# Dividing the last octet's head outputs instead of its softmax weights, with a new order of work

## The chip, the cores and the metric

The kernel runs on one core of one Trainium2 chip. The metric is the device time of one execution in microseconds (us), the median of several runs. Engines are named as the profile names them: PE (TensorE, matrix products; PEld is its weight load), DVE (VectorE), ACT (ScalarE), POOL (GpSimd) and SP (SyncE, which here issues nearly all DMAs). PSUM is the memory into which PE accumulates, in 8 banks; SBUF holds everything else.

## The reference, cut to what matters

A recurrent attention layer with 8 memory rows runs over 2048 tokens in 64 segments of 32, one after the other: each segment needs the memory that the one before it made. Beside it stands a gated feed-forward layer on the same tokens, and a gate mixes the two.

```python
for s in range(n_seg):                       # 64 segments, in order
    h = concatenate([mem, x[:, 32*s:32*s+32]])      # 8 + 32 = 40 rows, 640 wide
    q, k, v = h @ Wq, h @ Wk, h @ Wv         # 32 heads of 192
    scores = where(mask, q @ k.T * scale, -1e9)
    p = softmax(scores)                      # over 40 keys
    o = (p @ v) @ Wo                         # sum over the heads
    mem = o[:, :8]                           # the next segment's memory
    outs.append(o[:, 8:])
g = sigmoid((x * gate_w).sum(-1))
return g * concatenate(outs) + (1 - g) * (gelu(x @ w_gate) * (x @ w_up)) @ w_down
```

## The kernel before, in words

The feed-forward layer is done first, in about the first tenth of the time. The 64 segments follow, and this is what the change touches.

**Heads and octets.** The 32 heads are taken eight at a time: four *octets* per segment, numbered 0 to 3 in the order of work (even segments take the heads upwards, odd ones downwards). Weights do not all fit into SBUF. Of the pieces of the first and last octet, 13 of W_q, W_k and W_v (384 KB each) and 3 of W_o (480 KB each) share their places: when a piece has been used, SP loads its partner into the same place (`swap_loads`), for use later in the same segment. SP issues these DMAs in order, among its other loads and stores.

**Left rows.** The last 8 tokens of each segment do not depend on the memory. Their Q and K are computed for four segments and one octet at once (a *left group*: `left_mm`, LQ and LK), evicted by ACT (`left_rows`, L889), transposed by DVE (L891) and stored to DRAM; their V (`vl_mm`, Vl) and output product (`wo_left`, Wol) are likewise made for four segments at once. Which left group falls to a segment depends on its number modulo 4; segments with remainder 3 have none, but carry the Wol products, those with remainder 0 carry most of Vl.

**One octet's steps.** The projections (`proj`) are PE matmuls in groups of four that run side by side in 32-column tiles, k = 0 to 4 along the 640; ACT evicts rows and V, DVE transposes the rows of Q and K into place (`row_transp`, L1080), POOL adds the left rows (`left_fill`, L941 and L943). `scores` writes the mask and the products to a PSUM bank; DVE takes the maximum and subtracts it. `softmax`: ACT's exp (L1124), then on DVE the sum (L1126), its reciprocal (L1128), and two products that write p in two parts, 32 main keys (L1130) and 8 left keys (L1131). `p_transp` transposes p on PE (L1144, L1149); for the last octet ACT evicts the main part and DVE the other (L1158). `pv_oct` multiplies by V (L1177, L1179); ACT evicts the head outputs u (L1188), for the last octet DVE does a third of it (L1193); POOL copies the left rows of u aside (L1196). `wo_part` multiplies by W_o: octets 0 to 2 add up in one PSUM bank (L1206), whose two halves `half_sums` adds on ACT and DVE (L1212, L1215); the last octet has a bank of its own (L1229, twelve groups of four matmuls).

**End of a segment.** DVE adds the two (L1371), transposes the new memory into the next segment's input (L1375), in two parts each, and then mixes in the gate and the feed-forward part (L975). The next segment's first projection needs that transposition.

**Order.** Each engine executes its own instructions in the order in which the program adds them, and waits on semaphores that follow from the regions each step reads and writes (`_Sched`). The order is the list `PROG`, written out as a literal list, the same for all segments: ("g", n, k) a projection group of `GROUPS[n]`, ("tq" | "tk", o) the row transpositions, ("sc", o) scores, ("ex", o) softmax, ("pt", o) transposition of p, ("pv", o) the product with V, ("wo", o, half) the output product, ("lf" / "le", remainder, unit, k or m) a left group's matmuls and evictions in segments with that remainder, ("vb", k) the left V of the next segment. Left evictions that stand behind the last ("wo", 3, 1) are added after the end of the segment.

Of the kernel before, what the change touches and what calls it, by code (L numbers as in the profile page):

```python
# [3 lines left out]
ACTF = mybir.ActivationFunctionType  # L4
ALU = mybir.AluOpType
# [226 lines left out]
def _build(nc, A_x, A_mem0, A_Wq, A_Wk, A_Wv, A_Wo, seg_len, w_gate, w_up, w_down,  # L232
# [140 lines left out]
    r_ident = sreg(wsA_off["ident"], 256)  # L373
    maskm = bview(wsA_off["maskm"], R * 2)
# [125 lines left out]
    def piece_view(key, o):  # L500
        if key[0] == 3:
# [4 lines left out]
    PROG = [("g", 0, 0), ("g", 0, 1), ("g", 0, 2), ("g", 0, 3), ("g", 0, 4), ("tq", 0), ("g", 1, 0), ("tk", 0),  # L506
# [610 lines left out]
    def softmax(s, o):  # L1117
# [14 lines left out]
        if o == NOCT - 1:  # L1132
            for fn, rp in zip(fns, r_pp):
                S_.add("dve", fn, reads=[rb, rst], writes=[rp], name="smax p")
# [336 lines left out]
```

## Time and profile before

| | |
|---|---|
| median of 3 runs | 1765.9 us (1765.88 to 1769.65) |
| the profiled execution | 1766.88 us, span 1765.1 us |
| PE busy | 1623.9 us (92%) |
| DVE, ACT, POOL busy | 960.0, 802.8, 320.0 us (54%, 45%, 18%) |
| DMA | 499.57 MB, mean 283 GB/s |
| granted PE clock | 0.994 of full speed |

The span runs from the first to the last instruction of the profiled execution; the execution's own time is 1.8 us longer. Busy time is the union of an engine's instructions. "Idle before" is the time that an engine stood still just before an instruction, with what ended it.

### The profile page before, as it was taken

The page shows a single profiled execution, that of the slowest core. Times are in us where ns is not written, and L with a number is a line of the kernel's source. Part 1 is how long each engine was busy: PE and PEld are TensorE (multiplying, and loading weights), DVE is VectorE, ACT ScalarE, POOL GpSimd, SP SyncE. Part 2 cuts the span into 40 slices and gives each one's busy share as a digit, 9 for nine tenths or more (in the row PEclk, how much of TensorE's full clock was granted, in tenths as well). Part 3 has the DMA queues.
Part 4 walks back from the last instruction along what each step waited for, and adds up shares of the span by engine and source line. Part 5 has one row for each costly group of instructions (what it writes and reads, how often), then busy time and mean ns, then how long its engine had stood idle before and what let it go on. Part 6 is the DMA issues. An engine that isn't in the chain of part 4 may idle for free.

```text
span 1765.1 us, 80301 instructions
## 1 busy us (share of the span) xinstructions
PE 1623.9 (92%) x39162; PEld 809.5 (46%) x31501; DVE 960.0 (54%) x2932; ACT 802.8 (45%) x1835; POOL 320.0 (18%) x1099
## 2 busy tenths in 40 slices
PE   9999999999999999999999989999999998999887
PEld 4554444444444444454444444454444444454444
DVE  2222655556555655555555655555555655655554
ACT  3222544545444544444444544444444544445443
POOL 1100111111112112111212111111211121121211
PEclk9999999999999999999999999999999999999999
DMA  9814987888778887888788887879787886879776
GB/s 335 295 48 157 329 313 250 320 313 288 280 269 311 299 308 253 315 290 319 281 280 293 296 293 250 314 285 323 279 280 275 311 310 241 312 282 327 283 275 238
DMA packets 271311, 499.57 MB, mean 283 GB/s; under 512 B 105304, under 2 KB 132208, under 8 KB 270960
## 3 DMA queue, kind: packets, MB, share of 16 engines
q1 hardware_dynamic: 267832, 491.34, 78.3%
q8 instruction: 276, 4.52, 1.0%
q10 hardware_dynamic: 3128, 3.09, 0.6%
q14 instruction: 75, 0.61, 0.1%
HBM read 473.22 MB, written 21.11 MB: 280 GB/s over the span
## 4 chain that ended last, share of the span: by engine, by line
PE 71%; DVE 15%; DMA 6%; issue 4%; ACT 4%; DVEq 0%; SPq 0%; ACTq 0%
PE ps L1046 20%; PE ps L226 15%; PE ps L1206 8%; DMA arena<-in_A_Wo_dram 5%; PE ps L1177 3%; PE ps L804 3%; PE ps L801 3%; PE ps L884 3%; PE ps L1100 3%; PE ps L819 2%; PE ps L1087 2%; DVE ps L1114 2%; DVE arena L1112 2%; PE ps L1095 2%; PE ps L1229 2%
## 5 line engine op out<-in xcount | busy, mean ns | idle before, releaser
L1046 PE MATMUL ps<-arena 128*32 128x384 bf16 x9940 | 723.0, 329 | 42.4 <-DVE arena L1375 34.4
L226 PE MATMUL ps<-arena 128*32 128x384 bf16 x7680 | 595.4, 328 | 7.9 <-DVE arena L1215 3.5
L1046 PEld LDWEIGHTS ps<-arena 128*32 128x32 bf16 x9940 | 257.5, 97 | 365.3 <-issue 226.0
L1080 DVE STREAM_TRANSPOSE arena<-arena 128x384 bf16<-128x384 bf16 x512 | 270.8, 557 | 150.8 <-ACT arena L1066 149.2
L1066 ACT ACTIVATE arena<-ps 128x384 bf16<-128x384 f32 x512 | 236.2, 489 | 211.6 <-PE ps L1046 196.3
L1206 PE MATMUL ps<-arena 128*32 128x320 bf16 x6144 | 293.6, 301 | 13.9 <-issue 13.4
L1124 ACT ACTIVATE ps<-ps 104x160 f32<-104x160 f32 x256 | 71.9, 281 | 293.4 <-DVE ps L1114 293.4
L1206 PEld LDWEIGHTS ps<-arena 128*32 128x32 bf16 x6144 | 163.5, 97 | 74.0 <-issue 19.4
L1112 DVE TENSOR_REDUCE arena<-ps 104x4 f32<-104x160 f32 x256 | 83.0, 324 | 165.8 <-PE ps L1100 164.6
L941 POOL COPY arena<-arena 128x96 bf16<-128x96 bf16 x256 | 70.3, 275 | 513.4 <-PE ps L1100 444.2
L1188 ACT ACTIVATE arena<-ps 128x480 bf16<-128x480 f32 (+1 forms) x256 | 137.0, 535 | 43.8 <-PE ps L1179 39.6
L1196 POOL COPY arena<-arena 128x96 bf16<-128x96 bf16 x256 | 68.3, 267 | 441.1 <-ACT arena L1188 357.3
L1162 ACT ACTIVATE arena<-ps 128x448 bf16<-128x448 f32 x192 | 104.2, 543 | 96.7 <-PE ps L1149 96.4
L1069 ACT ACTIVATE arena<-ps 128x384 bf16<-128x384 f32 x256 | 125.1, 489 | 20.9 <-PE ps L1046 16.3
L1177 PE MATMUL ps<-arena 128*64 128x160 bf16 x1536 | 123.1, 243 | 12.5 <-ACT arena L1162 6.9
L1126 DVE TENSOR_REDUCE arena<-ps 104x4 f32<-104x160 f32 x256 | 83.0, 324 | 92.5 <-ACT ps L1124 92.5
L1177 PEld LDWEIGHTS ps<-arena 128*64 128x64 bf16 x1536 | 80.8, 109 | 91.6 <-issue 31.7
L884 PE MATMUL ps<-arena 128*32 128x384 bf16 x1280 | 111.4, 330 | 2.2 <-issue 2.0
L1179 PE MATMUL ps<-arena 128*64 128x64 bf16 x1536 | 104.8, 193 | 4.1 <-issue 4.1
L891 DVE STREAM_TRANSPOSE arena<-arena 128x384 bf16<-128x384 bf16 x128 | 73.7, 576 | 31.6 <-ACT arena L889 27.8
L1215 DVE TENSOR_TENSOR arena<-ps,arena 64x160 f32<-64x160 f32 x160 | 50.8, 317 | 72.3 <-ACT arena L1212 61.6
L1114 DVE TENSOR_TENSOR ps<-ps,arena 104x160 f32<-104x160 f32 x256 | 85.0, 332 | 8.8
(84 smaller groups left out, 1819.2 us busy)
## 6 DMA issues: line engine op xcount, KB each, us to landing
arena<-in_A_Wk_dram SPq DMA_DIRECT2D x335, 384.0 KB, 7.1
arena<-in_A_Wv_dram SPq DMA_DIRECT2D x335, 384.0 KB, 9.1
arena<-in_A_Wo_dram SPq DMA_DIRECT2D x205, 480.0 KB, 6.4
arena<-in_A_Wq_dram SPq DMA_DIRECT2D x209, 384.0 KB, 5.4
arena<-left_qk_scratch SPq DMA_DIRECT2D x126, 96.0 KB, 2.8
left_qk_scratch<-arena SPq DMA_DIRECT2D x49, 192.0 KB, 2.3
left_qk_scratch<-arena SPq DMA_DIRECT2D x30, 96.0 KB, 5.7
ffn_b_scratch<-arena ACTq DMA_DIRECT2D x16, 160.0 KB, 4.4
```

The source lines that it names most:

```text
L226: return e.add_instruction(mybir.InstMatmult(name=nm, start_tensor_calc=like["start"], stop_tensor_calc=stop, tile_size=(128, 32), tile_po ...
L884: fns.append(lambda e, outp=outp, rhs=rhs, j=j: e.matmul(outp, lhs, rhs, start=(k == 0), stop=(k == KT - 1), tile_position=(0, 32 * j)))
L1046: fns.append(lambda e, outp=outp, rhs=rhs, j=j: e.matmul(outp, lhs, rhs, start=(k == 0), stop=(k == KT - 1), tile_position=(0, 32 * j)))
L1066: S_.add("act", lambda e, m=m, bk=bk: e.activation(out=rows_sb[m], in_=ps[:, bk, 0:384], func=ACTF.Copy), reads=[r_ps[bk]], writes=[r_rows ...
L1069: S_.add("act", lambda e, i=i, bk=bk: e.activation(out=v_sb[i % NVB].rearrange("p (c n) -> p c n", c=3), in_=ps[:, bk, 0:384].rearrange("p ...
L1080: S_.add("dve", lambda e: e.transpose(out=dst[:, :, 0:L], in_=rows_sb[m].rearrange("p (c r) -> p c r", r=L)), reads=[r_rows[m]], writes=[r ...
L1112: S_.add("dve", lambda e: e.tensor_reduce(out=mxs, in_=S3, axis=AX.X, op=ALU.max), reads=[rb], writes=[rst], name="smax max")
L1114: S_.add("dve", lambda e: e.tensor_tensor(out=S3, in0=S3, in1=mxb, op=ALU.subtract), reads=[rb, rst], writes=[rb], name="smax sub")
L1177: return [lambda e: e.matmul(full, v[:, e0:e0 + 64], PTm[:, i], start=True, stop=False, tile_position=(0, 64 * i), skip_group_check=True), ...
L1179: lambda e: e.matmul(part, vl[:, e0:e0 + 64], PTl[:, i], start=False, stop=True, tile_position=(0, 64 * i), skip_group_check=True)]
L1188: S_.add("act", lambda e: e.activation(out=apx(u[:, 0, 0, :], [[R, na], [3 * R, 4], [1, R]]), in_=ps[:, A, 0:na * W].rearrange("p (c t r) ...
L1206: fns.append(lambda e, i=i, t=t, j=j, gv=gv: e.matmul(ps[32 * j:32 * j + 32, bank, 0:2 * DJ].rearrange("p (h n) -> p h n", h=2), lhs2[i], ...
```

## The change

For the last octet alone, exp now writes p itself, unnormalised, in its two parts (two ACT instructions); the DVE sum, reciprocal and products of that octet are gone. A column of ones (beside the mask in SBUF) times the transposed p gives each row's sum on PE, in every one of the 64 rows that the head outputs of that tile take ("PVn"). DVE takes the reciprocal of these sums, 128x160, from PSUM into the place of K's rows. The product with V is split into two PE steps (PVa, PVb), and DVE evicts both with a multiplication by the reciprocals ("uT norm", 128x320; "uT norm2", 128x160), where ACT and DVE each copied one before. POOL's copy of the left rows follows both. The last octet's W_o matmuls are ordered by the thirds c of a head pair: c = 0 and 1 of a half's pairs first, and c = 2 of all four pairs at the very end. The half sums of octets 0 to 2 become an item of the order, ("hs", 0), which stands behind ("pv", 3). `PROG` is new throughout.

```diff
--- before.py
+++ after.py
@@ -371,6 +371,10 @@
     r_gallL = sreg(wsA_off["gallL"], 128)
     ident = bview(wsA_off["ident"], 256)
     r_ident = sreg(wsA_off["ident"], 256)
+    assert R * 2 + 2 <= wsA["maskm"]
+    ones = bview(wsA_off["maskm"] + R * 2, 2).broadcast_to([128, 64])
+    r_ones = sreg(wsA_off["maskm"] + R * 2, 2)
+    rcp, r_rcp = fview(wsB_off["K"], 16 * R), sreg(wsB_off["K"], 16 * R)
     maskm = bview(wsA_off["maskm"], R * 2)
     r_maskm = sreg(wsA_off["maskm"], R * 2)
 
@@ -503,20 +507,20 @@
         return bview(o, GQ)
 
     GROUPS = [[(0, 0), (1, 0)], [(2, 0), (0, 1), (1, 1)], [(2, 1), (0, 2)], [(1, 2)], [(2, 2), (0, 3)], [(1, 3)], [(2, 3)]]
-    PROG = [("g", 0, 0), ("g", 0, 1), ("g", 0, 2), ("g", 0, 3), ("g", 0, 4), ("tq", 0), ("g", 1, 0), ("tk", 0),
-            ("g", 1, 1), ("g", 1, 2), ("sc", 0), ("g", 1, 3), ("ex", 0), ("g", 1, 4), ("tq", 1), ("g", 2, 0),
-            ("g", 2, 1), ("g", 2, 2), ("lf", 1, 0, 0), ("pt", 0), ("g", 2, 3), ("tk", 1), ("g", 2, 4), ("g", 3, 0),
-            ("sc", 1), ("g", 3, 1), ("lf", 1, 0, 1), ("g", 3, 2), ("ex", 1), ("g", 3, 3), ("g", 3, 4), ("g", 4, 0),
-            ("lf", 1, 0, 2), ("pv", 0), ("lf", 1, 0, 3), ("g", 4, 1), ("tk", 2), ("g", 4, 2), ("pt", 1), ("g", 4, 3),
-            ("tq", 2), ("g", 4, 4), ("sc", 2), ("ex", 2), ("lf", 1, 0, 4), ("pv", 1), ("g", 5, 0), ("le", 1, 0, 0),
-            ("g", 5, 1), ("lf", 0, 1, 0), ("g", 5, 2), ("wo", 0, 0), ("le", 1, 0, 1), ("tq", 3), ("pt", 2), ("g", 5, 3),
-            ("wo", 0, 1), ("g", 5, 4), ("pv", 2), ("tk", 3), ("lf", 0, 1, 1), ("lf", 1, 1, 0), ("wo", 1, 0), ("sc", 3),
-            ("lf", 2, 1, 0), ("wo", 1, 1), ("g", 6, 0), ("lf", 2, 1, 1), ("lf", 1, 1, 1), ("g", 6, 1), ("ex", 3),
-            ("g", 6, 2), ("wo", 2, 0), ("lf", 1, 1, 2), ("pt", 3), ("g", 6, 3), ("lf", 2, 1, 2), ("g", 6, 4),
-            ("wo", 2, 1), ("lf", 2, 1, 3), ("lf", 1, 1, 3), ("pv", 3), ("lf", 0, 1, 2), ("lf", 2, 1, 4), ("lf", 1, 1, 4),
-            ("vb", 0), ("le", 1, 1, 0), ("vb", 1), ("vb", 2), ("vb", 3), ("le", 1, 1, 1), ("le", 2, 1, 0),
-            ("lf", 0, 1, 3), ("lf", 0, 1, 4), ("wo", 3, 0), ("le", 2, 1, 1), ("le", 0, 1, 0), ("wo", 3, 1), ("le", 0, 1, 1),
-            ("vb", 4)]
+    PROG = [("g", 0, 0), ("g", 0, 1), ("g", 0, 2), ("g", 0, 3), ("g", 0, 4), ("tq", 0), ("g", 1, 0), ("g", 1, 1),
+            ("tk", 0), ("g", 1, 2), ("sc", 0), ("g", 1, 3), ("ex", 0), ("g", 1, 4), ("g", 2, 0), ("g", 2, 1),
+            ("tq", 1), ("g", 2, 2), ("g", 2, 3), ("tk", 1), ("pt", 0), ("g", 2, 4), ("sc", 1), ("ex", 1),
+            ("pv", 0), ("lf", 1, 0, 0), ("g", 3, 0), ("g", 3, 1), ("lf", 1, 0, 1), ("g", 3, 2), ("lf", 1, 0, 2),
+            ("g", 3, 3), ("g", 3, 4), ("tq", 2), ("tk", 2), ("g", 4, 0), ("g", 4, 1), ("g", 4, 2), ("pt", 1),
+            ("g", 4, 3), ("g", 4, 4), ("g", 5, 0), ("g", 5, 1), ("sc", 2), ("lf", 1, 0, 3), ("lf", 1, 0, 4),
+            ("lf", 0, 1, 0), ("ex", 2), ("pv", 1), ("lf", 0, 1, 1), ("le", 1, 0, 0), ("le", 1, 0, 1), ("tq", 3),
+            ("wo", 0, 0), ("pt", 2), ("g", 5, 2), ("g", 5, 3), ("g", 5, 4), ("wo", 0, 1), ("wo", 1, 0), ("pv", 2),
+            ("tk", 3), ("sc", 3), ("wo", 1, 1), ("lf", 1, 1, 0), ("g", 6, 0), ("wo", 2, 0), ("lf", 2, 1, 0),
+            ("g", 6, 1), ("ex", 3), ("lf", 1, 1, 1), ("pt", 3), ("lf", 2, 1, 1), ("lf", 2, 1, 2), ("g", 6, 2),
+            ("lf", 1, 1, 2), ("g", 6, 3), ("lf", 0, 1, 2), ("g", 6, 4), ("wo", 2, 1), ("pv", 3), ("lf", 1, 1, 3),
+            ("vb", 0), ("lf", 1, 1, 4), ("vb", 1), ("lf", 0, 1, 3), ("hs", 0), ("lf", 2, 1, 3), ("lf", 2, 1, 4),
+            ("le", 1, 1, 0), ("le", 1, 1, 1), ("lf", 0, 1, 4), ("le", 0, 1, 0), ("vb", 2), ("vb", 3), ("wo", 3, 0),
+            ("le", 2, 1, 0), ("wo", 3, 1), ("vb", 4), ("le", 0, 1, 1), ("le", 2, 1, 1)]
     assert NOCT == 4
     WOP = 4
     NWP = NT
@@ -648,6 +652,7 @@
                                                  base=base, channel_multiplier=cm), reads=[reg], writes=[reg])
 
     S_.add("pool", lambda e: e.memset(maskm, 0.0), writes=[r_maskm])
+    S_.add("pool", lambda e: e.memset(bview(wsA_off["maskm"] + R * 2, 2), 1.0), writes=[r_ones])
     asel(maskm[:, 0:XA], r_maskm, [[-1, XA]], 0, 1, NEG)
     asel(maskm[:, L:R], r_maskm, [[-1, M]], -L, 1, NEG)
     asel(maskm[:, L:R], r_maskm, [[0, M]], -L, 1, 0.0)
@@ -1121,6 +1126,13 @@
         rst = r_st[o % 2]
         rcb = rcs.rearrange("p (t o) -> p t o", o=1).broadcast_to([104, 4, R])
         rb = r_ps[bank]
+        if o == NOCT - 1:
+            q = s % 4
+            for dst, src, rp in ((pm_sb[0:104], S3[:, :, 0:L], r_pp[0]),
+                                 (pl_sb[0:104, :, M * q:M * q + M], S3[:, :, L:R], r_pp[1])):
+                S_.add("act", lambda e, dst=dst, src=src: e.activation(out=dst, in_=src, func=ACTF.Exp, bias=0.0, scale=scale),
+                       reads=[rb], writes=[rp], name="smax exp")
+            return
         S_.add("act", lambda e: e.activation(out=S3, in_=S3, func=ACTF.Exp, bias=0.0, scale=scale),
                reads=[rb], writes=[rb], name="smax exp")
         S_.add("dve", lambda e: e.tensor_reduce(out=sms, in_=S3, axis=AX.X, op=ALU.add),
@@ -1129,11 +1141,7 @@
         q = s % 4
         fns = [lambda e: e.tensor_tensor(out=pm_sb[0:104], in0=S3[:, :, 0:L], in1=rcb[:, :, 0:L], op=ALU.mult),
                lambda e: e.tensor_tensor(out=pl_sb[0:104, :, M * q:M * q + M], in0=S3[:, :, L:R], in1=rcb[:, :, L:R], op=ALU.mult)]
-        if o == NOCT - 1:
-            for fn, rp in zip(fns, r_pp):
-                S_.add("dve", fn, reads=[rb, rst], writes=[rp], name="smax p")
-        else:
-            S_.add("dve", fns, reads=[rb, rst], writes=[r_p], name="smax p")
+        S_.add("dve", fns, reads=[rb, rst], writes=[r_p], name="smax p")
 
     def p_transp(s, o):
         bank = 5 + o % 2
@@ -1179,6 +1187,34 @@
                     lambda e: e.matmul(part, vl[:, e0:e0 + 64], PTl[:, i], start=False, stop=True,
                                        tile_position=(0, 64 * i), skip_group_check=True)]
 
+        if o in USPLIT:
+            def sums(i):
+                return [lambda e: e.matmul(ps[64 * i:64 * i + 64, B, 0:W], ones, PTm[:, i], start=True, stop=False,
+                                           tile_position=(0, 64 * i), skip_group_check=True),
+                        lambda e: e.matmul(ps[64 * i:64 * i + 64, B, 0:W].rearrange("p (t r) -> p t r", r=R)[:, :, XA:R], ones,
+                                           PTl[:, i], start=False, stop=True, tile_position=(0, 64 * i), skip_group_check=True)]
+
+            def both(x, y):
+                return [z for xy in zip(x, y) for z in xy]
+
+            vr = [r_v[o % NVB], r_vl[oc], r_PT]
+            S_.add("pe", both(sums(0), sums(1)), reads=[r_PT, r_ones], writes=[r_ps[B]], name="PVn s%d o%d" % (s, o))
+            S_.add("dve", lambda e: e.reciprocal(out=rcp, in_=ps[:, B, 0:W]), reads=[r_ps[B]], writes=[r_rcp], name="PV rcp s%d" % s)
+            S_.add("pe", both(half(0, 0), half(0, 1)) + both(half(1, 0), half(1, 1)), reads=vr, writes=[r_ps[A]], name="PVa s%d o%d" % (s, o))
+            S_.add("pe", both(half(2, 0), half(2, 1)), reads=vr, writes=[r_ps[B]], name="PVb s%d o%d" % (s, o))
+            S_.add("dve", lambda e: e.tensor_tensor(
+                out=apx(u[:, 0, 0, :], [[R, 2], [3 * R, 4], [1, R]]),
+                in0=ps[:, A, 0:2 * W].rearrange("p (c t r) -> p c t r", t=4, r=R), in1=apx(rcp, [[0, 2], [R, 4], [1, R]]),
+                op=ALU.mult), reads=[r_ps[A], r_rcp], writes=[ru[0]], name="uT norm s%d o%d" % (s, o))
+            S_.add("dve", lambda e: e.tensor_tensor(
+                out=u[:, :, 2, :], in0=ps[:, B, 2 * W:3 * W].rearrange("p (t r) -> p t r", r=R),
+                in1=rcp.rearrange("p (t r) -> p t r", r=R), op=ALU.mult),
+                reads=[r_ps[B], r_rcp], writes=[ru[1]], name="uT norm2 s%d o%d" % (s, o))
+            q = s % 4
+            S_.add("pool", lambda e: e.tensor_copy(
+                out=uTl[:, 12 * oc:12 * oc + 12, M * q:M * q + M].rearrange("p (t c) i -> p t c i", c=3), in_=u[:, :, :, L:R]),
+                reads=[r_uT[o % NUB]], writes=[r_uTl[oc]], name="uTl s%d o%d" % (s, o))
+            return
         fns = [x for c in range(3) for y in zip(half(c, 0), half(c, 1)) for x in y]
         if s % 4 == 0:
             S_.add("pe", fns[:2], reads=[r_v[o % NVB], r_PT], writes=[r_ps[A]], name="PV s%d o%d" % (s, o))
@@ -1216,6 +1252,8 @@
                 out=zsum[64 * h:64 * h + 64], in0=ps[0:64, bank, DJ * h:DJ * (h + 1)], in1=zpart[0:64, DJ * h:DJ * (h + 1)],
                 op=ALU.add), reads=[r_ps[bank], r_zp], writes=[r_zp], name="Zs " + tag)
 
+    late_wo = []
+
     def wo_part(s, item):
         ub = item[1] % NUB
         u = uT[ub]
@@ -1224,21 +1262,22 @@
         allp = wo_pairs(s, ("wo", NOCT - 1)) if lasto else [p for i in range(NOCT - 1) for p in wo_pairs(s, ("wo", i))]
         held = [(p,) + piece(s, (3, p)) for p in pairs]
         if lasto:
-            for p, g_, rg_ in held:
-                for c in range(3):
-                    S_.add("pe", [lambda e, j=j, c=c, g_=g_, p=p: e.matmul(
-                        ps[32 * j:32 * j + 32, OB2, SC:512], u[:, p % 4, c, 0:L], g_[:, c, DJ * j:DJ * (j + 1)],
-                        start=(p == allp[0] and c == 0), stop=(p == allp[-1] and c == 2),
-                        tile_position=(0, 32 * j)) for j in range(4)],
-                        reads=[rg_, r_uT[ub]], writes=[r_ps[OB2]], name="Wo s%d p%d" % (s, p))
+            late_wo.extend(held)
+            end = pairs[-1] == allp[-1]
+            for c, (p, g_, rg_) in [(c, x) for c in range(2) for x in held] + [(2, x) for x in late_wo if end]:
+                S_.add("pe", [lambda e, j=j, c=c, g_=g_, p=p: e.matmul(
+                    ps[32 * j:32 * j + 32, OB2, SC:512], u[:, p % 4, c, 0:L], g_[:, c, DJ * j:DJ * (j + 1)],
+                    start=(p == allp[0] and c == 0), stop=(p == allp[-1] and c == 2),
+                    tile_position=(0, 32 * j)) for j in range(4)],
+                    reads=[rg_, r_uTp[ub][c // 2]], writes=[r_ps[OB2]], name="Wo s%d p%d" % (s, p))
+            if end:
+                late_wo.clear()
             return held
         for (pa, ga, ra), (pb, gb, rb) in zip(held[::2], held[1::2]):
             for c in range(3):
                 S_.add("pe", wo_split(OB, [u[:, pa % 4, c, 0:L], u[:, pb % 4, c, 0:L]], [ga[:, c, :], gb[:, c, :]],
                                       pa == allp[0] and c == 0, pb == allp[-1] and c == 2),
                        reads=[ra, rb, r_uT[ub]], writes=[r_ps[OB]], name="Wo s%d p%d" % (s, pa))
-        if pairs[-1] == allp[-1]:
-            half_sums(OB, "s%d" % s)
         return held
 
     def wo_left(s, held):
@@ -1251,7 +1290,7 @@
 
     assert PROG.index(("g", [n for n, ms in enumerate(GROUPS) if (2, 1) in ms][0], KT - 1)) < PROG.index(("wo", 0, 0))
     late_at = ("g", 1, KT - 1)
-    items = [item for item in PROG if item[0] not in ("lf", "le", "vb")]
+    items = [item for item in PROG if item[0] not in ("lf", "le", "vb", "hs")]
     n_wo = PROG.index(items[-1])
     assert PROG.index(("sc", 2)) < PROG.index(("pv", 1))
     assert wsB["K"] >= 768
@@ -1331,6 +1370,8 @@
                     for m in range(2):
                         LBK[m] = lb[item[2], m]
                     left_mm(*unit(s, item[2]), item[3], unit_piece)
+            elif kind == "hs":
+                half_sums(OB, "s%d" % s)
             elif kind == "vb":
                 if q == 3 and g + 1 < NG:
                     if i == 0:
```

## The prediction, made before the result was known

> **What bounds the kernel now.** I read the page first, then the groups of instructions with shapes kept apart, the list of waits, and the chain of waits across the end of one segment. The page:
>
> ```profile
> PE 1623.9 (92%) x39162; PEld 809.5 (46%) x31501; DVE 960.0 (54%) x2932; ACT 802.8 (45%) x1835; POOL 320.0 (18%) x1099
> ```
>
> TensorE is busy 92% of the span, so a shorter VectorE chain pays only where TensorE waits for it. The waits (engine and line, what it waited for, us in total, times, longest):
>
> ```profile
> PEld ps L1144 <- DVE arena L1131: 84.6, 155, 1.0
> ...
> PE ps L1046 <- DVE arena L1375: 34.4, 48, 1.2
> PE ps L1144 <- DVE arena L1131: 25.0, 65, 0.7
> ...
> PE ps L1229 <- DMA arena<-in_A_Wo_dram: 6.1, 10, 2.3
> ```
>
> L1144 is the transposition of p, L1375 the new memory's transposition that lets the next segment begin. In the trace the 64 segments start (first Q matmul, L1046) on average 24.70 us apart: by number mod 4, called the kind from here, 25.16, 25.07, 23.42 and 25.21 for kinds 0 to 3. Now the chain of waits across the end of a kind 2 segment (start, us, what):
>
> ```profile
> 939.32 0.59 DVE arena L891
> ...
> 940.01 0.58 DVE arena L891
> 940.59 0.16 DVE arena L1371
> ...
> 940.77 0.26 DVE arena L1375
> ...
> 941.07 0.35 PE ps L1046 x4
> ```
>
> and two lines of the timeline of the same stretch:
>
> ```profile
> 938.95 0.31 DVE L1193 CAST arena<-ps 128x160 bf16<-128x160 f32 x1
> 939.32 1.13 PE L1229 MATMUL ps<-arena 128*32 128x160 bf16 x48
> ```
>
> The last 48 output matmuls end at 940.45, yet L1371, which adds them up, starts at 940.51: VectorE's two left transposes (L891) ran until 940.58. VectorE's in-order queue already touches the end of a segment, and there the change puts its new work.
>
> Prices of VectorE's operations (mean ns after the count and busy time):
>
> ```profile
> L1131 DVE TENSOR_TENSOR arena<-ps,arena 104x32 bf16<-104x32 f32 x256 | 46.2, 180 | 0.0
> L1130 DVE TENSOR_TENSOR arena<-ps,arena 104x128 bf16<-104x128 f32 x256 | 74.6, 291 | 10.4
> L809 DVE TENSOR_TENSOR arena<-ps,arena 128x512 bf16<-128x512 f32 x48 | 33.2, 691 | 70.6 <-PE ps L804 68.0 <-ACT arena L807 2.6
> L1128 DVE RECIPROCAL arena<-arena 104x4 f32<-104x4 f32 x256 | 45.6, 178 | 8.8
> L1114 DVE TENSOR_TENSOR ps<-ps,arena 104x160 f32<-104x160 f32 x256 | 85.0, 332 | 8.8
> L1215 DVE TENSOR_TENSOR arena<-ps,arena 64x160 f32<-64x160 f32 x160 | 50.8, 317 | 72.3 <-ACT arena L1212 61.6 <-PE ps L1179 5.6 <-PE ps L1206 1.6
> L891 DVE STREAM_TRANSPOSE arena<-arena 128x384 bf16<-128x384 bf16 x128 | 73.7, 576 | 31.6 <-ACT arena L889 27.8
> ```
>
> **Removed ahead of the last transposition of p.** Sum 0.32, reciprocal 0.18 and two products 0.29 + 0.18 leave VectorE; ScalarE writes p in two exps in place of one 0.28 (104x128 and 104x32, some 0.25 and 0.18). From scores to that transposition the chain falls from 2.6 to 1.6 us. TensorE waited there 0.29, 0.14, 0.20 and 0.01 us by kind (start of L1144 less the previous group's pitch): worth 0.16 on average, for the rest was covered.
>
> **Order ahead of the last P.V.** Scores and P.V now often stand together; each switch from 32-wide tiles to them costs about 0.10 (0.26 between starts in place of 0.16), and 1 or 2 of 7 vanish: -0.15. First transposition after four matmul groups of g2 in place of three: its waits of 0.28 and 0.26 (kinds 2, 3) go, -0.12. Kind 1's wait of 0.51 before the third P.V goes, -0.13. Against this: the second scores follow g2 at once, and K's transposition ends 6.97 us into a kind 2 segment and TensorE now arrives at 6.8: 0.1 to 0.2 with the hop in all kinds but 0, +0.10. The third transposition of p needs 2.64 us after its scores; ahead of it the old order had 1.76 us in kind 2, the new has 0.40 + 0.42 + 0.42, so the wait grows from 0.86 to 1.40; likewise kind 3 from 0.37 to 1.0, kinds 0 and 1 by 0.1 to 0.2: +0.36. In kind 1 two left transposes (2 x 0.58) now stand between p and the last Q and K transposes: scores wait 0.5 there, less kind 2's old 0.26, +0.06. One left group (0.33) moves behind P.V in kinds 1 and 2, one ahead in kind 0: -0.08; kind 0's sums also wait for V's bank, +0.03. Sum: P.V starts 0.09, rounded 0.1 us, earlier than now.
>
> **Added from P.V on.** Sums: four matmuls, a third of P.V's 0.42: 0.14. Then VectorE alone, in order: reciprocal of 128x160, product of 128x320 (691 - 192 x 1.04 = 0.49; 1.04 ns an element from 291 to 691 over 384), product of 128x160 (0.33). Before, ScalarE did 0.44 and VectorE 0.31 side by side. The half sums, now emitted behind these, add 2 x 0.32, and a left transpose 0.58 stands ahead of the end in kinds 0 and 2, two in kind 1.
>
> The reciprocal has no row of this size. L1128 does 4 elements in 178 ns. Lower end: all excess is fixed, 178 + 156 x 1.04 = 0.34 us. Upper: L1131, the nearest in size, has 180 - 33 = 147 ns fixed; the rest, 31 ns, is 7.8 an element, 1.39 us. From L1130's fixed 158 it is 5 an element, 0.96. I take 1.39 by the nearest row.
>
> [...]
>
> From the start of the sums to the next segment: 0.14 + hop 0.10 + 1.39 + 0.04 + 0.49 + 0.03 + 0.33 = 2.52. Kinds 0 and 2: + half sums 0.70 + left transpose 0.61 + L1371 and L1375 with hops 0.55 = 4.38. Kind 1 has one more transpose: 4.99. Kind 3 has none, but there TensorE's left outputs now wait for POOL's copy of both products (L1196, 0.27): 2.52 + 0.10 + 0.27 + 0.10 + 0.40 + 0.56 + 0.20 + 0.55 = 4.70. Mean 4.61. Now the same stretch is 3.57, 3.86, 3.35 and 3.70, mean 3.62. So +0.99 - 0.10 = +0.89 a segment, times 64 = 57 us. TensorE's side, two left groups or four Vl groups (0.66) as cover, ends sooner (3.85), so the extra matmuls cost no more than their 0.14.
>
> The profiled execution took 1766.9 (span 1765.1), 1.0 over the median: 1766.9 + 57 - 1 = 1823.
>
> Costed at nothing: the first queue of the next segment. Kind 2's second left transpose and its store move behind the end, so SP reaches the next segment's weights about 1.1 us later (first swap 1.62 us after the start in kind 1, where this is so now, against 0.54). Kind 3 needs its last W_o piece at 24.0 and has it at 21.5: cover 2.4. If that were gone, 0.5 x 16 = 8 us. The last pieces also face more matmuls behind them: seven groups of 0.07 follow the last landing in place of three, 0.28, covered while VectorE ends later.
>
> **Rivals.** *Cheap reciprocal*: 0.34 us. VectorE's tail falls by 1.05 to 3.56, so -0.06 - 0.10 = -0.16 a segment, -10 us: 1756; up to 20 us better if the third wait for p grows less than I count. For it: TensorE then meets the products in time, and the reciprocal's excess may be a fixed one. Against: 31 ns for 4 elements. It decides from below 1.39 - 0.89 = 0.50 us. *Half-dear reciprocal*: 0.96 us, +0.46, 29 us: 1795. *Weights late*: the last W_o piece of kind 1 lands 23.67 us into a segment and is used at 23.72, so with a cheap reciprocal kind 1 can't gain and the delayed kind 3 loses its 0.5; 10 us less gain: 1766.
>
> **How the numbers follow.** Dear reciprocal 0.50, half-dear 0.13, cheap 0.30, weights late 0.07. About 0.3% (5 us) is what a measurement can tell from no change. Faster: most of the cheap case with its margin, 0.30; same: 0.06; slower 0.64. The dear case's own range is 1800 to 1836 (0.3 us a segment either way on the order); for 8 in 10 the range takes in the half-dear and most of the cheap: 1748 to 1836.
>
> **What would show it.** Right: a reciprocal of 128x160 at 1.2 to 1.5 us 64 times, TensorE's W_o matmuls of the last octet waiting for the first product, L1371 starting right behind VectorE's left transpose, few waits before the last transposition of p, more before the third. Wrong: a reciprocal under 0.5 us; or the third transposition's wait unchanged; or W_o matmuls that wait for DMA.

## The result, and the profile after

The changed kernel takes 1839.1 us (median of 4 runs, 1837.1 to 1840.5) against 1766.9 us before (median of 4): a ratio of 1.040, 95% interval 1.038 to 1.043, or 72 us slower. The forecast was 1823, with 1836 as the top of its range: the result lies above both. The sign and the main mechanism, VectorE's longer queue at the end of a segment, came out as predicted; the size was 16 us short, and the part of the sum that was wrong is the one ahead of the last P.V.

The page of the profile, engines and the waits of TensorE after (engine and line, what it waited for, us in total, times, longest):

```profile
span 1837.9 us, 80549 instructions
...
PE 1614.0 (88%) x39418; PEld 832.2 (45%) x31757; DVE 1007.5 (55%) x2804; ACT 773.3 (42%) x1835; POOL 319.4 (17%) x1100
```

```profile
PEld ps L1152 <- DVE arena L1143: 78.9, 143, 1.0
...
PE ps L1185 <- DVE arena L1202: 58.2, 62, 1.1
...
PE ps L1051 <- DVE arena L1416: 35.7, 48, 1.2
PE ps L1152 <- DVE arena L1143: 33.5, 60, 0.8
...
PE ps L1100 <- DVE arena L1085: 15.3, 33, 0.8
...
PEld ps L1268 <- DMA arena<-in_A_Wo_dram: 11.3, 17, 1.6
```

TensorE's busy time is nearly that of before (1614.0 us against 1623.9), now 88% of a longer span: it waits. One wait is new and is the largest of PE's: L1185, the third part of P.V, stands 58 us for L1202, the reciprocal. The transposition of p (L1152, L1144 before) waits 33.5 us in 60 places where it waited 25.0 in 65, though the last octet's is gone from it. Scores (L1100) wait for row transposes (L1085). The next segment's wait for the memory (L1051 for L1416; before L1046 for L1375, 34.4) hardly moved.

The new instructions, in the groups with shapes apart (count | busy us, mean ns of one | idle before):

```profile
L1202 DVE RECIPROCAL arena<-ps 128x160 f32<-128x160 f32 x64 | 74.1, 1158 | 79.4 <-PE ps L1194 79.4
...
L1140 DVE RECIPROCAL arena<-arena 104x4 f32<-104x4 f32 x192 | 34.2, 178 | 6.6
...
L1205 DVE TENSOR_TENSOR arena<-ps,arena 128x320 bf16<-128x320 f32 x64 | 31.5, 492 | 6.0 <-PE ps L1187 2.3
...
L1209 DVE TENSOR_TENSOR arena<-ps,arena 128x160 bf16<-128x160 f32 x64 | 20.1, 315 | 0.8 <-PE ps L1187 0.6
```

The end of a kind 2 segment, as the chain of waits has it (start, us, what):

```profile
974.02 1.17 DVE arena L1202
...
975.24 0.26 PE ps L1185 x2
...
975.52 0.28 PE ps L889 x4
975.80 0.16 PE ps L226 x4
975.96 0.19 PE ps L889 x4
...
976.24 0.50 ACT arena L894
...
976.76 0.59 DVE arena L896
977.35 0.25 DVE arena L1412
...
977.63 0.26 DVE arena L1416
...
977.93 0.35 PE ps L1051 x4
```

and in the timeline of the same stretch:

```profile
973.78 0.20 PE L1194 MATMUL ps<-arena 128*64 128x64 bf16 x2
...
974.02 1.16 DVE L1202 RECIPROCAL arena<-ps 128x160 f32<-128x160 f32 x1 [1.45 <-PE ps L1194]
...
975.22 0.49 DVE L1205 TENSOR_TENSOR arena<-ps,arena 128x320 bf16<-128x320 f32 x1
...
975.24 0.26 PE L1185 MATMUL ps<-arena 128*64 128x160 bf16 x2 [0.91 <-DVE arena L1202]
...
975.62 0.31 DVE L1209 TENSOR_TENSOR arena<-ps,arena 128x160 bf16<-128x160 f32 x1
...
975.97 0.67 DVE L1251 TENSOR_TENSOR arena<-ps,arena 64x160 f32<-64x160 f32 x2
...
976.12 1.11 PE L1268 MATMUL ps<-arena 128*32 128x160 bf16 x48
```

The reciprocal holds two things at once. On VectorE the products and half sums queue behind it. On TensorE the third part of P.V goes into the bank that the sums occupy. Its columns are others (320 to 479, the sums' are 0 to 159), but the kernel tracks PSUM by whole banks (`r_ps`), so its semaphore holds P.V back until the reciprocal has read the sums; the left group behind it (L889, L226), its eviction (L894) and its transposition (L896) are late by that too. Both paths reach L1412 nearly together: W_o ends at 977.23, L896 at 977.34. VectorE has 0.12 us of slack between the half sums and L896.

From the trace, per segment on average (us). A *wait* here is the time from the start of the previous matmul group to the start of this one, less its usual pitch (the time between the two starts where nothing waits); *work* is the period less all waits.

| | before | after |
|---|---|---|
| period | 24.70 | 25.83 |
| start of the segment to start of sums or P.V of the last octet | 21.10 | 21.28 |
| from there to the next segment | 3.60 | 4.55 |
| work | 20.96 | 20.92 |
| waits, all | 3.74 | 4.91 |
| third part of P.V, for the reciprocal | 0 | 1.07 |
| third transposition of p | 0.56 | 0.85 |
| last transposition of p | 0.16 | 0.00 |
| first transposition of p | 0.14 | 0.01 |
| second scores | 0 | 0.22 |
| last scores (kind 1 alone) | 0.08 (0.04) | 0.25 (0.91) |
| sums | – | 0.14 |
| K and V projections | 0.13 | 0.31 |
| W_o of the last octet | 0.53 | 0.24 |

1.13 us a segment times 64 is 72 us. 0.95 of it lie behind the start of the sums, as forecast (0.99); 0.17 lie ahead of it, where the forecast had a gain of 0.10.

### The profile page after: what moved, and what is told of

The parts are those of the page before. It is cut to its first block, busy times and chain, and to the rows that moved or that the text cites. A ratio compares the mean times of both kernels' runs of the same rounds, so it can differ in the third digit from the quotient of the medians.

```text
span 1837.9 us, 80549 instructions
## 1 busy us (share of the span) xinstructions
PE 1614.0 (88%) x39418; PEld 832.2 (45%) x31757; DVE 1007.5 (55%) x2804; ACT 773.3 (42%) x1835; POOL 319.4 (17%) x1100
## 3 DMA queue, kind: packets, MB, share of 16 engines
q8 instruction: 278, 4.55, 1.0%
## 4 chain that ended last, share of the span: by engine, by line
PE 64%; DVE 19%; DMA 8%; issue 4%; ACT 4%; DVEq 0%; ACTq 0%; SPq 0%; POOL 0%; POOLq 0%
PE ps L1051 18%; PE ps L226 12%; PE ps L1242 9%; DMA arena<-in_A_Wk_dram 4%; DVE arena L1202 3%; PE ps L809 3%; DMA arena<-in_A_Wo_dram 3%; PE ps L1185 3%; PE ps L806 3%; PE ps L889 3%; DVE arena L1085 3%; PE ps L1105 3%; PE ps L1100 2%; DVE arena L896 2%; PE ps L824 2%
## 5 line engine op out<-in xcount | busy, mean ns | idle before, releaser
L1051 PE MATMUL ps<-arena 128*32 128x384 bf16 x9940 | 701.2, 328 | 49.8 <-DVE arena L1416 35.7
L226 PE MATMUL ps<-arena 128*32 128x384 bf16 x7680 | 585.1, 327 | 6.1 <-DVE arena L1251 3.5
L1051 PEld LDWEIGHTS ps<-arena 128*32 128x32 bf16 x9940 | 260.5, 97 | 401.2 <-issue 255.7
L1085 DVE STREAM_TRANSPOSE arena<-arena 128x384 bf16<-128x384 bf16 x512 | 272.6, 559 | 145.9 <-ACT arena L1071 144.1
L1071 ACT ACTIVATE arena<-ps 128x384 bf16<-128x384 f32 x512 | 237.6, 492 | 198.9 <-PE ps L1051 187.7
L1185 PE MATMUL ps<-arena 128*64 128x160 bf16 x1536 | 129.7, 244 | 66.3 <-DVE arena L1202 58.2
L1117 DVE TENSOR_REDUCE arena<-ps 104x4 f32<-104x160 f32 x256 | 83.0, 324 | 184.4 <-PE ps L1105 184.4
L946 POOL COPY arena<-arena 128x96 bf16<-128x96 bf16 x256 | 69.5, 272 | 614.5 <-PE ps L1105 528.7
L1074 ACT ACTIVATE arena<-ps 128x384 bf16<-128x384 f32 x256 | 124.9, 488 | 48.1 <-PE ps L1051 45.1
L1136 ACT ACTIVATE ps<-ps 104x160 f32<-104x160 f32 x192 | 54.0, 281 | 202.6 <-DVE ps L1119 202.6
L1185 PEld LDWEIGHTS ps<-arena 128*64 128x64 bf16 x1536 | 80.9, 108 | 116.0 <-DVE arena L1202 67.4
L1224 ACT ACTIVATE arena<-ps 128x480 bf16<-128x480 f32 x192 | 108.8, 567 | 58.4 <-PE ps L1187 58.2
L1202 DVE RECIPROCAL arena<-ps 128x160 f32<-128x160 f32 x64 | 74.1, 1158 | 79.4 <-PE ps L1194 79.4
L889 PE MATMUL ps<-arena 128*32 128x384 bf16 x1280 | 109.7, 329 | 2.3 <-issue 2.3
L1187 PE MATMUL ps<-arena 128*64 128x64 bf16 x1536 | 109.8, 193 | 1.1 <-issue 1.0
L1232 POOL COPY arena<-arena 128x96 bf16<-128x96 bf16 x192 | 51.3, 267 | 333.4 <-ACT arena L1224 329.2
L894 ACT ACTIVATE arena<-ps 128x384 bf16<-128x384 f32 x128 | 57.4, 488 | 101.1 <-PE ps L889 90.2
L1138 DVE TENSOR_REDUCE arena<-ps 104x4 f32<-104x160 f32 x192 | 62.3, 324 | 68.6 <-ACT ps L1136 67.8
```

The costliest lines, as they stand in the source:

```text
L226: return e.add_instruction(mybir.InstMatmult(name=nm, start_tensor_calc=like["start"], stop_tensor_calc=stop, tile_size=(128, 32), tile_po ...
L889: fns.append(lambda e, outp=outp, rhs=rhs, j=j: e.matmul(outp, lhs, rhs, start=(k == 0), stop=(k == KT - 1), tile_position=(0, 32 * j)))
L1051: fns.append(lambda e, outp=outp, rhs=rhs, j=j: e.matmul(outp, lhs, rhs, start=(k == 0), stop=(k == KT - 1), tile_position=(0, 32 * j)))
L1071: S_.add("act", lambda e, m=m, bk=bk: e.activation(out=rows_sb[m], in_=ps[:, bk, 0:384], func=ACTF.Copy), reads=[r_ps[bk]], writes=[r_rows ...
L1074: S_.add("act", lambda e, i=i, bk=bk: e.activation(out=v_sb[i % NVB].rearrange("p (c n) -> p c n", c=3), in_=ps[:, bk, 0:384].rearrange("p ...
L1085: S_.add("dve", lambda e: e.transpose(out=dst[:, :, 0:L], in_=rows_sb[m].rearrange("p (c r) -> p c r", r=L)), reads=[r_rows[m]], writes=[r ...
```

## The experiments

Twelve variants, four to a session; each ratio is to the kernel before in its own session (1769.6, 1760.7 and 1761.3 us for the three fours). Period, waits and work are us per segment from the profiled execution.

| run | median us | ratio, 95% | period | waits | work |
|---|---|---|---|---|---|
| after | 1839.1 | 1.040, 1.038–1.043 | 25.83 | 4.91 | 20.92 |
| e1 new order, old normalisation | 1799.0 | 1.016, 1.008–1.023 | 25.27 | 4.48 | 20.79 |
| e2 new normalisation, old order | 1894.4 | 1.071, 1.064–1.078 | 26.71 | 5.62 | 21.09 |
| e3 thirds in one bank | 1830.1 | 1.034, 1.027–1.040 | 25.60 | 4.68 | 20.92 |
| e4 copy for reciprocal | 1802.1 | 1.018, 1.012–1.024 | 25.29 | 4.35 | 20.94 |
| e5 half sums early | 1900.9 | 1.080, 1.076–1.083 | 26.66 | 5.74 | 20.92 |
| e6 = e3 + half sums early | 1874.2 | 1.064, 1.061–1.067 | 26.46 | 5.51 | 20.95 |
| e7 = e6 + sums early | 1825.0 | 1.036, 1.033–1.039 | 25.60 | 4.57 | 21.03 |
| e8 = e7 in the old order | 1811.3 | 1.029, 1.025–1.032 | 25.25 | 4.05 | 21.20 |
| e9 = e3 + sums early | 1812.1 | 1.029, 1.024–1.034 | 25.51 | 4.49 | 21.02 |
| e10 = after, old order up to the last scores | 1829.5 | 1.038, 1.032–1.043 | 25.76 | 4.67 | 21.09 |
| e11 = e9, old order up to the last scores | 1798.9 | 1.021, 1.017–1.025 | 25.22 | 4.02 | 21.20 |
| e12 = e9, old order throughout | 1805.8 | 1.025, 1.020–1.030 | 25.41 | 4.22 | 21.19 |

### e1 and e2: the two halves of the change

e1 keeps the new `PROG` and the new order within W_o, and takes the old normalisation back:

```diff
-        if o == NOCT - 1:
-            for dst, src, rp in (...): S_.add("act", ... Exp ...)
-            return
...
-            S_.add("pe", both(sums(0), sums(1)), ... name="PVn s%d o%d" % (s, o))
-            S_.add("dve", lambda e: e.reciprocal(out=rcp, in_=ps[:, B, 0:W]), ...)
```

> The new order and the new W_o order with the normalised p and the two plain evictions of before; nothing else of the change. Theory (the reciprocal on the path is most of the loss, and the order alone costs some 17 us): TensorE's wait of 1.07 us before the third part of P.V goes, but the last transposition of p waits 0.3 to 1.1 us for the full softmax, which the new order no longer covers: 1800 to 1825 us. Rival (the order is harmless, all of the loss is the division): 1757 to 1777 us. Rival (the order is the loss): about 1839 us.

e2 is the reverse: the new normalisation in the old list, with the half sums in the place where the old kernel made them.

```diff
-            ("wo", 2, 1), ("lf", 2, 1, 3), ("lf", 1, 1, 3), ("pv", 3), ...
+            ("wo", 2, 1), ("hs", 0), ("lf", 2, 1, 3), ("lf", 1, 1, 3), ("pv", 3), ...
```

> The new normalisation in the old order, with the half sums behind wo(2,1) as before. Theory: the wait for the reciprocal stays at about 1.0 us a segment and the losses of the order (0.27 us ahead of P.V) go: 1815 to 1828 us. Rival (the new order is what pays for the division): slower than 1839 us. Rival (the order is the loss): 1765 to 1780 us.

The order alone costs 1.6% (0.8 to 2.3), some 27 us, just under the range expected of it; its tail is the old one (3.61 us against 3.60). So the order is slower by what stands ahead of P.V: the third transposition waits 0.82, the second scores 0.21, the last scores 0.25 (0.89 in kind 1), and now the last transposition 0.42, where one projection group less stands beside the old chain from scores to it. The 0.26 that are new there do not occur in the changed kernel, so the 27 us are the price of the order with the old softmax. Only work falls, by 0.17: the vanished shape switches (forecast 0.15). Weights also come later than they are wanted; TensorE's waits in e1:

```profile
PE ps L1149 <- DVE arena L1136: 33.1, 59, 0.8
PE ps L1237 <- DMA arena<-in_A_Wo_dram: 18.9, 20, 2.2
```

The second was 6.1 us before. The rest, 4.0% less 1.6%, some 44 us, is what the new normalisation adds in this order.

e2 missed its forecast by 66 us or more. The wait of P.V's third part rose to 1.75: the half sums on VectorE, now ahead of the reciprocal in its queue, wait for ScalarE's part, and the reciprocal waits behind them. By its number e2 fits the rival that the new order pays for the division. But e5 below has the same edits in the new order and is no faster (1.080 against 1.071), so the place of the half sums made e2 slow, not the old order.

### e3 and e4: the bank or the reciprocal

e3 puts the third part of P.V into the bank of the other two:

```diff
-                full = ps[64 * i:64 * i + 64, B if c == 2 else A, W * c:W * c + W]
+                full = ps[64 * i:64 * i + 64, A, W * c:W * c + W]
...
-                in0=ps[:, B, 2 * W:3 * W]...
+                in0=ps[:, A, 2 * W:3 * W]...
```

> The changed kernel, but the last third of P.V is written to the bank of the other two, so it no longer waits until the reciprocal has read the sums' bank. Theory A (TensorE's wait for that bank sets the end of a segment): 0.5 us a segment less, about 1805 us. Theory B (VectorE's queue of reciprocal, products, half sums and left transposes sets it, and TensorE's wait lies beside it): only kind 3 gains, 1828 to 1835 us.

e4 takes the reciprocal's price away; it leaves the division out, so its outputs are multiplied by the sums:

```diff
-            S_.add("dve", lambda e: e.reciprocal(out=rcp, in_=ps[:, B, 0:W]), ...
+            S_.add("dve", lambda e: e.tensor_copy(out=rcp, in_=ps[:, B, 0:W]), ...
```

> The changed kernel with a copy in place of the last octet's reciprocal, so the sums multiply where their reciprocals should: the division is left out. A copy of this size takes 0.31 us, the reciprocal took 1.16. Theory (the reciprocal's length is on the path all along): 0.85 us a segment less unless the weights then come too late, 1785 to 1795 us. Rival (the order and the queue behind are the loss): 1820 us or more.

Waits of TensorE in e3:

```profile
PE ps L1268 <- DVE arena L1205: 38.4, 57, 1.5
PE ps L1051 <- DVE arena L1416: 37.7, 48, 1.4
```

The wait of 58.2 us at L1185 is gone, and L1268 (W_o of the last octet) now waits 38.4 us for the first product, L1205. Per segment 1.07 us less at P.V, 0.76 more at W_o. So TensorE's largest wait was mostly a symptom: it sat in front of VectorE's queue in another place. By the medians some 9 us are its own, by the profiles 14 (25.83 to 25.60; e3's profile is of its fastest run), and the intervals, 1.027–1.040 and 1.038–1.043, overlap. That is Theory B of the expectation, VectorE's queue.

e4's copy takes 325 ns in place of 1158, 0.83 us a segment or 53 us; the time fell by 37 us. The wait at P.V shrinks to 0.26, W_o of the last octet rises to 0.45, of it in kind 1 to 1.37, and there it waits for its weights:

```profile
PE ps L1268 <- DMA arena<-in_A_Wo_dram: 18.7, 24, 1.7
```

7.7 us in the kernel after. The time lies between theory and rival: the reciprocal's length counts, but not all of it. Even with a reciprocal as cheap as a copy, the change is 32 us slower than before (1.8%, 1.2 to 2.4).

### e5 and e6: half sums ahead of the reciprocal

```diff
-            ..., ("wo", 2, 1), ("pv", 3), ..., ("lf", 0, 1, 3), ("hs", 0), ("lf", 2, 1, 3), ...
+            ..., ("wo", 2, 1), ("hs", 0), ("pv", 3), ..., ("lf", 0, 1, 3), ("lf", 2, 1, 3), ...
```

> The changed kernel with the half sums of octets 0 to 2 back behind wo(2,1), ahead of P.V, so that 0.64 us leave VectorE's queue behind the reciprocal. Theory A (TensorE's wait for the sums' bank sets the end): no change, 1836 to 1841 us. Theory B (VectorE's queue sets it): up to 0.6 us in kinds 0 and 1, 1815 to 1825 us. If both end at nearly the same time: 1830 to 1836 us.

e6 has e3's edit as well.

> Both: the last third of P.V in the bank of the other two, and the half sums ahead of P.V. If the two queues run neck and neck to the end of a segment, this gains more than the two alone together: some 0.55 us a segment, about 1802 us. Theory A alone: as with the bank alone, 1805 us. Theory B alone: as with the half sums alone, 1815 to 1825 us.

Both came out far slower than any expectation. VectorE's own waits and TensorE's in e5:

```profile
DVE arena L1251 <- ACT arena L1248: 83.6, 59, 3.4
```

```profile
PE ps L1185 <- DVE arena L1202: 109.2, 62, 2.0
```

and the timeline of one such end:

```profile
1298.64 0.20 PE L1194 MATMUL ps<-arena 128*64 128x64 bf16 x2
1298.77 0.43 ACT L1248 ACTIVATE arena<-ps 64x320 f32<-64x320 f32 x1
...
1299.31 0.67 DVE L1251 TENSOR_TENSOR arena<-ps,arena 64x160 f32<-64x160 f32 x2 [1.56 <-ACT arena L1248]
1299.90 1.14 DVE L1202 RECIPROCAL arena<-ps 128x160 f32<-128x160 f32 x1
```

The sums are done by 1298.84, the reciprocal starts at 1299.90. In between VectorE first stands idle for ScalarE's half (L1248) and then does the half sums. Per segment the wait at P.V rises from 1.07 to 1.86, which is 51 of the 53 us by which the profiled span grew (1890.4 less 1837.9; this was e5's fastest run, by the medians it is 62). I had counted the half sums as 0.65 us of free time ahead of the reciprocal; in an in-order queue their own input decides, and it comes late. In e6 the same delay sits in front of W_o (1.61 us). In the new order the change's place for the half sums, behind P.V, is thus the better one.

### e7 to e9: the sums as soon as p is there

The ones need only the transposed p, not V. In these the sums and the reciprocal are an item of their own, right behind the last projection group ("g", 6, 4), with P.V's thirds in one bank:

```diff
-            ("lf", 0, 1, 2), ("g", 6, 4), ("wo", 2, 1), ...
+            ("lf", 0, 1, 2), ("g", 6, 4), ("pn", 3), ("wo", 2, 1), ...
...
+            elif kind == "pn":
+                pv_sums(s, i)       # sums into a bank of their own, reciprocal
```

e7 and e8 have the half sums early, e9 as in the change; e8 is in the old order.

> The kernel with bank and half sums mended, and in addition the sums and their reciprocal right behind the last projection group, ahead of wo(2,1) and P.V, so that the reciprocal runs beside TensorE's work. Theory (only the reciprocal's place costs): its 1.16 us leave the path but for some 0.3, 1750 to 1770 us, where the last W_o pieces from DRAM begin to set the end. Rival (the products and the order cost as much): 1790 us or more.

> The same in the old order: sums and reciprocal behind the last projection group, thirds in one bank, half sums behind wo(2,1). Theory: as before the change, less the 0.16 us that TensorE waited for the last p, plus 0.14 us of matmuls and some wait for the products: 1760 to 1775 us. Rival (the new order pays once the reciprocal is hidden): slower than the new order with the same edits.

> Sums and reciprocal behind the last projection group and thirds in one bank, as in the run before the last, but the half sums left behind P.V as in the change. Theory (half sums in front of VectorE's queue wait for ScalarE and hold what stands behind them: there the reciprocal, here the products): the wait for the products falls by about 0.5 us a segment, 1785 to 1805 us. Rival (the products or the W_o pieces from DRAM are late anyway): 1815 us or more.

e7 gained 49 us on e6; e9 gained half a per cent on e3, with overlapping intervals. Against what the theory forecast they came out late by 55 us (e7), 36 (e8) and 7 (e9). With the same edits the old order is the faster one (e8 against e7, intervals apart). In e9 the wait for the product at W_o fell as meant:

```profile
PE ps L1275 <- DMA arena<-in_A_Wo_dram: 17.0, 21, 2.1
...
PE ps L1275 <- DVE arena L1212: 7.5, 17, 1.2
```

7.5 us for the product, from e3's 38.4; but 17.0 us for W_o's pieces (10.8 in e3), 1.63 us per segment of kind 1. Here DMA takes over as the last to be ready. Work rises by 0.10 against e3 (21.02 and 20.92): the sums stand away from P.V and pay a shape switch, the 0.10 that the prediction read from the trace (0.26 us between starts in place of 0.16).

### e10 to e12: which part of the order

e10 is the change with the old list up to ("sc", 3), e11 the same with e9's edits, e12 the old list throughout with e9's edits.

```diff
+    PROG = <before's items up to ("sc", 3)> + <the other items in the order of after>
```

> The changed kernel with the old order up to the last scores and the new order from there. Theory (the new middle costs by itself: the third transposition of p, the second and the last scores wait 0.68 us more a segment, of which 0.13 and 0.16 come back elsewhere): some 0.3 to 0.4 us a segment less, 1812 to 1822 us. Rival (what is saved in the middle is waited for at the end): 1834 to 1842 us.

> Both: the old order up to the last scores, the new one from there, with sums and reciprocal behind the last projection group, thirds in one bank and half sums behind P.V. Theory (reciprocal's place and middle add up): 1765 to 1785 us. Rival: within 10 us of the better of the two before.

> The old order throughout, with sums and reciprocal behind the last projection group, thirds in one bank and the half sums behind P.V and the first left groups. Theory (as for the new order: half sums no longer ahead of the products): 0.4 us a segment less than with the half sums in front, 1780 to 1790 us. Rival: no change from 1811 us.

All three came out above their forecasts, by 7, 14 and 16 us. e12 cannot be told from e8 (1.020–1.030 against 1.025–1.032), nor from e9, so in the old order the place of the half sums is not shown to matter. In e10 the waits ahead of the last scores return to the old ones (third transposition 0.48, second scores 0, last scores 0.08), the first transposition's comes back (0.16), and work rises by 0.17, the shape switches. Net 0.06 us a segment, 4 us, within the interval of no difference to after. So undoing the new middle does not give back what its waits add up to. Part of the reason is on TensorE's list of waits: rare stalls of up to 2 us for which the profile names no releaser ("issue") make up 33.9 us before, 34.9 after, and 48.9 in e10 (25.1 of them at W_o, L1229; before 13.4, L1206), 0.2 us a segment more. What they are is not shown. With the sums early the old middle is worth more, 0.29 us a segment by the profiles (25.51 to 25.22), 13 us by the medians (e9's profile is of its slowest run); why more there than in e10 is not shown.

e11 is the best version found with the new normalisation, and 2.1% (1.7 to 2.5) slower than before. Its work closes: 20.96 + 0.14 for the sums' matmuls + 0.10 for their switch is 21.20. Its waits are 0.28 above before: sums 0.13 (they follow p closely), K and V projections 0.26, W_o of the last octet 0.08, less 0.16 at the last transposition; all other items together come to -0.03. So in e11 the new normalisation, with the order that goes with it, pays 0.24 in work and more in new waits for the 0.16 us of waiting that it removes. Of the K and V projections' 24 us in all, some 15 are the "issue" stalls (46.5 us of them in the whole of e11) and some 4 are DMA (1.2 us at L1038 for W_k in PE's list). No version beat the kernel before.

## Why the prediction was right in its mechanism and wrong in its size

**The tail: right in the mean.** Forecast 3.62 to 4.61 us, measured 3.60 to 4.55. By kind 4.38, 4.99, 4.38, 4.70 were forecast; 4.20, 4.90, 4.15, 4.95 came. Products 0.49 and 0.33 measured 0.492 and 0.315.

**The reciprocal: dear, but mis-sized.** 1.39 us was taken, 1.158 measured, between the row taken and the 0.96 of the other. The per-element price, estimated from the two measured reciprocals, is (1158 - 178) / 156 = 6.28 ns. With it the tail's sum by kind would have been 4.15, 4.76, 4.15 and 4.47. Kinds 0 and 2 came within 0.05 of that. Kind 1 is 0.14 longer (W_o waits 0.67 there) and kind 3 is 0.48 longer: there TensorE, late by 1.24 at P.V's third part, has the left outputs still to do, and waits only 0.28 for the memory at the end. So part of the agreement in the mean is luck: two errors that cancel.

**"TensorE's side … ends sooner (3.85), so the extra matmuls cost no more than their 0.14": reason wrong, conclusion nearly right.** The step overlooked that P.V's third part shares a bank with the sums and must wait for the reciprocal: 1.07 us in every segment. e3 shows that this wait, taken away, is mostly handed to W_o.

**Ahead of P.V: the step that failed.** The sum of "Order ahead of the last P.V" had P.V start 0.10 earlier; it starts 0.17 later. 0.27 times 64 is 17 us, and the miss is 16. Removing the normalisation was worth what was said (last transposition 0.16), so were the first transposition (0.14 to 0.01, forecast 0.12), the shape switches (work -0.17 in e1, forecast 0.15) and nearly the third transposition (+0.29, forecast +0.36). Too small were the second scores (+0.22, forecast +0.10) and the last scores (+0.17, forecast +0.06: 0.91 us in kind 1, forecast 0.5); the third P.V's wait in kind 1 fell from 0.51 to 0.30 and did not vanish. Not foreseen were the sums' own wait (0.14, of which 0.03 was counted) and the K and V projections' (+0.18). Of the last, the total wait for W_k from DMA, 5.5 us after and 0.5 before, is the kind that "the first queue of the next segment" costed at nothing; some 9 us more of them are "issue" stalls, which fell on other matmuls before. These misses come to 0.60, less 0.07 at the third transposition; what is over 0.27 came back in items not forecast, 0.10 of it at W_o of octet 2. The table tells where the time went, not what each wait would give back: e10 undid the waits at the second and last scores and the third transposition and got 0.06 us.

**The range.** "0.3 us a segment either way on the order" is 19 us, so the dear case's range would be 1804 to 1842 and not 1800 to 1836. The order's miss of 0.27 lies within the 0.3 that the prediction itself allowed; the top that it wrote down does not follow from it.

**The rival of a cheap reciprocal: its price was wrong.** "It decides from below 0.50 us" with 1756 as its time. e4 has 0.325 us in that place and takes 1802. The same step fails: the sum believed that without the tail the change gains, while its order alone loses 1.6% (e1). In e4 the sums start 0.36 later than forecast (21.36 us into a segment against 21.00), and the tail is 0.37 longer than the rival's 3.56, most of all in kind 1 (4.58). *Weights late* was right as a mechanism, and not as a price: in e4 W_o of kind 1 waits 1.37 us for its pieces, in e9 1.63.

**The signs named.** The reciprocal is 1.16 us, just short of the 1.2 to 1.5 named; fewer waits before the last transposition and more before the third: right. L1412 (L1371 before) starts right behind the left transpose in the stretch shown (977.34): right. "W_o matmuls of the last octet waiting for the first product" showed only once the bank was out of the way (38.4 us in e3, also in e6 and e7); in the changed kernel the wait sits one step earlier. Of the signs against it, W_o's wait for DMA rose a little (7.7 us in PE's list, 6.1 before).

## What to carry to other kernels

Price a change of order by itself: here the list alone, with the old softmax, cost some 27 us where the whole change cost 72, and it showed as five waits of 0.1 to 0.3 us, none of them large. Before a wait is blamed, ask what the next engine will wait for once it is gone: 1.07 us removed at P.V came back as 0.76 at W_o, and a reciprocal cheaper by 53 us gave 37. In an in-order queue a short instruction whose input is late costs its wait, not its length: two half sums of 0.65 us put ahead of the reciprocal cost 53 us by the profiles.

## What the hardware showed

**VectorE's reciprocal of 128x160 from PSUM took 1158 ns** (mean of 64), where a copy of the same 128x160 from PSUM took 325 (e4) and the reciprocal of 104x4 from SBUF 178. From the two reciprocals, 980 ns apart over 156 more elements of a row, the price of an element is estimated at 6.28 ns, six times the 1.04 ns an element between the products of 128 and 512 elements (291 and 691 ns).

**TensorE's granted clock was half in some stretches in the middle of the work.** Its mean over the span was 0.975 in e5 and 0.994 in the changed kernel and before. For e5 that makes an estimate of some 95 us at half (0.025 x 1890.4 x 2). In the changed kernel the half-clock stretches add up to 23 us: they start at 1418.81, 1524.62, 1579.23, 1630.43 and 1804.51 us, 31, 16, 15 and 51 times 3.413 us apart, and last 3.41 us (the third 6.83); a last one takes the 2.67 us before the end of the span. In the 3.41 us ahead of the five PE was busy 1.42, 1.49, 1.64, 1.63 and 2.05 us (42, 44, 48, 48 and 60%). Not each such stretch is followed by one: after those that start at 589.40, 1053.60, 1159.40 and 1756.70, with PE busy 1.76, 1.78, 1.76 and 1.72 us (50 to 52%), the clock stayed full. Windows of e5 (window, length, busy us and count of PE, PEld, DVE, ACT and POOL, granted clock, DMA share, GB/s):

```profile
1294.72:1298.13 3.41, 3.21 (x96) 2.06 (x88) 1.09 (x4) 0.80 (x3) 0.27 (x1) 1.00 0.87 222
1298.13:1301.54 3.41, 1.51 (x40) 0.80 (x32) 2.16 (x5) 0.92 (x2) 0.29 (x1) 1.00 0.87 327
1301.54:1304.95 3.41, 2.78 (x68) 1.85 (x56) 2.05 (x7) 0.87 (x2) 1.15 (x3) 0.50 0.02 4
```

The 1.9 us that P.V waits fall into the second window; PE is busy 1.51 us of it, and the third is granted half. In the changed kernel's longest half-clock stretch the projection groups start 0.32 us apart (at 1583.00, 1583.32, 1583.64 and 1583.96, for instance), and 0.16 apart once the clock is full again (1586.14 and 1586.30). How much of the half clock reached the end of a segment is not shown; apart from P.V's, e5's waits and its work add up to those of the changed kernel (24.80 and 24.76 us a segment).
